# GpSimd masks one score tile of four ahead of its exponential and makes low words; the remaining keys' values come first; the scale moves into query evictions

## The chip, the cores and the metric

The kernel runs on one core of one Trainium2 chip. The metric is device time in microseconds. Three timed runs of the kernel before gave 1319.81, 1322.06 and 1323.58 us; the median, 1322.06, is the time to be changed. One further execution was profiled.

In the text, PE is TensorE (PEld its weight loads), DVE is VectorE, ACT is ScalarE, POOL is GpSimd, and SP is the engine whose queue issues nearly all the DMAs. L468 means line 468 of the kernel before.

## The reference

Two layers follow each other. The first is attention in which only scores within tau of their row's maximum count; the second is a feed-forward block with a squared ReLU. All data that the kernel computes with is fp32, but the two weight matrices arrive as 64-bit floats.

```python
# q, k, v: (8, 8, 576, 64) fp32; tau = 0.02
scores = matmul(q, k^T) / 8
thresh = max(scores, axis=-1) - tau
scores = where(scores >= thresh, scores, -1e9)
attn = exp(scores - max(scores))
attn = attn / (sum(attn) + 1e-9)
x = matmul(attn, v)                    # -> reshaped to (4608, 512)
h = maximum(x @ w_in, 0)               # w_in  (512, 2048)
out = (h * h) @ w_out                  # w_out (2048, 512)
```

## The kernel before, in words

**Two stages.** Attention comes first and leaves its result, transposed, in DRAM. The feed-forward stage (hidden layer on L828, output layer on L963, both with a seven-product scheme over 2 x 2 blocks) reads it back. The change touches attention alone.

**Units and periods.** There are 32 pairs of heads. A *unit* is 128 query rows of one pair (two heads, j = 0 and 1); 576 = 4 x 128 + 64, so the last 64 rows of two neighbouring pairs share a unit. That makes 144 units. Function `period(p)` handles two of them, A = 2p and B = 2p + 1, in 72 full periods. Each unit has two score tiles of 128 x 576, one for each head, so a period has four: A0, A1, B0, B1. Work of three ages meets in a period: scores and softmax of A and B, transposes of the weights of the two units before (V and W), and the rest of the transposes (U) and the values product (PV) of the two units before those.

**The order is written out by hand.** The strings PLAIN (L607) and CONVERTING (L611) list the steps of a period; each engine executes its own steps in that order, one after the other, and semaphores tie the engines together. CONVERTING is used in periods 2 to 34, in which one weight chunk of 128 x 512 64-bit floats is turned into fp32 in each period; PLAIN is used elsewhere. The steps are:

| step | engine | what it does | line |
|---|---|---|---|
| SA, SB | PE | scores of unit A (with both units' last 64 keys), then of B | L436 |
| T, eT | PE, ACT | transposes of queries and keys of a coming pair, and their evictions | L399, L404 |
| topA0 ... topB1 | DVE | scores times -1/8 (qscale) out of PSUM into tile s, and their minimum | L453 |
| leastA, leastB | POOL | thresholds: minimum plus tau, 128 x 2 | L460 |
| powA0 ... | ACT | exponential of tile s into tile w | L463 |
| maskA0 ... | DVE | w = (s <= threshold) * w, and its sum | L468 |
| over, inv, spread | POOL, DVE, POOL | sum + 1e-9, reciprocal, and its spreading to 128 x 256, for the units before | L475, L478, L512 |
| U, V, W and eU, eV, eW | PE, ACT | transposes of the weights, and their evictions | L381, L526 |
| PV | PE | values product into PSUM banks 0 and 5 | L551 |
| x | DVE | PV's result times the reciprocal; its stores and coming loads of values are issued behind it | L653 |
| s1, s2 | POOL | one sum of two weight blocks each (128 x 512), from period 35 on, while there are any; s2 only up to period 59 | L122, L125 |
| c1 to c6 | ACT, ACT, POOL, DVE, DVE, POOL | conversion of a chunk: absolute value of the high words, low words to a float's size, clamp, shift, combine, add | L205, L212, L219, L227, L235, L245 |

Before the change c3 to c6 belong to the chunk of the period before.

**What ties the steps.** Scores of a period use the same PSUM banks as PV's result and the tops of the period before: banks 0 and 5 hold tiles A0 and A1 and then PV's result, so SA waits for x. Banks 1 and 4 hold the last 64 keys' scores and the transposes T, so topA0 waits for T, and eT for the tops. Tile s has two buffers, one each for A and B; w has four. U's transposes read w of two periods before, and so a step that writes w waits for U. Function `touch` (L356) keeps these orders by banks. The transposes use one PSUM tile of two banks, so U waits for eV of the period before and V for eU.

**PV's order.** The product adds up five blocks of keys: four of 128 and one of 64 (FULL), in the order 0, 1, FULL, 2, 3. A product over 128 keys uses PE tiles of 128 x 64, one over 64 keys tiles of 64 x 64, the same as scores.

Of the kernel before, what the change touches and what calls it, by code (L numbers as in the profile page):

```python
# [12 lines left out]
U32 = mybir.dt.uint32  # L13
ALU = mybir.AluOpType
# [34 lines left out]
def kernel(  # L49
# [25 lines left out]
    nc = tc.nc  # L75
# [133 lines left out]
    def convert2(m):  # L209
        if m in parts:  # L210
            lo = parts[m][0]
            nc.scalar.activation(out=lo, in_=lo.bitcast(U32), func=AF.Copy, bias=0.0, scale=2.0**-29)  # L212
# [179 lines left out]
    def turn(i, which, spots, other=None):  # L392
# [13 lines left out]

        def then():
            if which:
                blocks = to[1].rearrange("p (t q) -> p t q", q=HALF)
                evicted(nc.scalar.copy, blocks[:, 0::2, :], spots[0], 0, half + REST)  # L410
                evicted(other if other else nc.scalar.copy, blocks[:, 1::2, :], spots[1], 0, half)
                evicted(nc.scalar.copy, to[2].rearrange("p (t q) -> p t q", q=HALF), spots[1], half, REST)
                next_keys(i)
            else:
                for r in range(2):
                    part = to[0][:, ds(r * half, half)].rearrange("p (t q) -> p t q", q=HALF)
                    evicted(nc.scalar.copy, part, spots[r], 0, half)
                if i + 1 < len(pairs):
                    load_q(i + 1)
# [20 lines left out]

    def softmax(n):
# [9 lines left out]
        def top(j):  # L451
            at = 3 * j * BANK + (n % 2 != j) * (2 * BANK - REST)
            made = nc.vector.tensor_scalar(  # L453
                out=s[:, j, :], in0=sc[:, ds(at, S)], scalar1=qscale[:, :], scalar2=None,
                op0=ALU.mult, op1=ALU.min, accum_out=nmx[:, j : j + 1],
            )
            touch("tops", made, at, S)
# [3 lines left out]

        def power(j):
            nc.scalar.activation(  # L463
                out=w[:, int(n % 2 != j), :], in_=s[:, j, :], func=AF.Exp, bias=nmx[:, j : j + 1], scale=-1.0
            )

        def mask(j):
            nc.vector.scalar_tensor_tensor(  # L468
                out=w[:, int(n % 2 != j), :], in0=s[:, j, :], scalar=thr[:, j : j + 1], in1=w[:, int(n % 2 != j), :],
                op0=ALU.is_le, op1=ALU.mult, accum_out=sm[:, j : j + 1],  # L470
            )
# [8 lines left out]
        soft[n] = dict(top=top, least=least, power=power, mask=mask, over=over, inverse=inverse)  # L480
# [58 lines left out]
    def values(m):  # L539

        for n, c in enumerate((0, 1, FULL, 2, 3)):
# [62 lines left out]
    def begun(n):  # L604
        return starts.get(n)

    PLAIN = """  # L607
        SA c3 T topA0 over U eU s1 SB topA1 powA1 leastA topB0 powB0 c1 s2 PV c4 V fetch
        inv spread powA0 c5 topB1 powB1 eT maskA1 x W eV maskA0 leastB c2 c6 eW maskB0 maskB1
    """.split()  # L610
    CONVERTING = """  # L611
        fetch c3 SA c1 SB topA1 over s1 U topA0 c2 powA1 topB0 topB1 eU leastA maskA1
        leastB inv spread powA0 PV powB0 W maskA0 x powB1 maskB0 T c4 c5 maskB1 eT V c6 eW eV
# [8 lines left out]
    def period(p):  # L622
# [51 lines left out]
        def every(key):  # L674
# [17 lines left out]
        for letter, n in (("A", A), ("B", B_)):  # L692
            for what, name in (("least", "least"),):
                steps[what + letter] = lambda n=n, name=name: do(n, name)
            for what, name in (("top", "top"), ("pow", "power"), ("mask", "mask")):
                for j in range(2):
                    steps[f"{what}{letter}{j}"] = lambda n=n, name=name, j=j: do(n, name, j)
# [528 lines left out]
```

## Time and profile before

| | us |
|---|---|
| median of three timed runs (1319.81 to 1323.58) | 1322.06 |
| profiled execution, whole time | 1318.88 |
| profiled execution, its span | 1317.1 |
| PE busy (matmuls) | 1275.0 |
| DVE busy | 1027.7 |
| ACT busy | 843.7 |
| POOL busy | 883.7 |
| first matmul of the feed-forward stage starts | 522.9 |

The granted TensorE clock was 0.999 of full speed over the whole execution.

How to read it: busy times are those of one execution and averages over stages with different limits. Matmuls are pipelined and the profile models their ends, so that a busy PE is not yet a full PE. A group's line gives busy time, the mean of one in ns, and the engine's idle time just before the group with what ended it. In a timeline, start and length come first; a record that is longer than its kind usually is was held up after it began. Spans on POOL are rough.

### The profile page before, as it was taken

Reading aid. Unit: us, or ns where it says so; the run is one execution under the profiler, and the core shown is the slowest. Engines: PE = TensorE matmul, PEld = TensorE weight load, DVE = VectorE, ACT = ScalarE, POOL = GpSimd, SP = SyncE. Lnnn points to the kernel's source line nnn. Section 1 sums busy time; section 2 is a strip of 40 time slices with the busy share of each in tenths; the row PEclk is TensorE's granted clock in tenths of the full one; section 3 lists DMA queues with packets and bytes.
Section 4 is the critical chain, followed back from the end, with each engine's and each line's share of the span. In section 5 each row is a group of like instructions: output and inputs, shape, how many; then the busy total and the mean of one; then the engine's idle time right before and its main releaser. Section 6 shows DMA issues by size and latency. Waiting matters only on the chain.

```text
span 1317.1 us, 40939 instructions
## 1 busy us (share of the span) xinstructions
PE 1275.0 (97%) x16059; PEld 1116.0 (85%) x16059; DVE 1027.7 (78%) x2497; ACT 843.7 (64%) x1464; POOL 883.7 (67%) x1030
## 2 busy tenths in 40 slices
PE   7898888899999999999999999999999999999998
PEld 5665656566666666999999999999999999999998
DVE  6999999999999997777877787777656644665463
ACT  5999999888988886466756675665524322432240
POOL 1555555566666431778977897768777777777775
PEclk9999999999999999999999999999999999999999
DMA  5454566543433321466556655659745134523411
GB/s 146 128 161 134 156 176 178 152 109 95 112 78 89 79 60 46 135 217 193 184 177 216 193 187 179 204 215 392 266 161 159 50 114 161 161 59 104 161 34 33
DMA packets 251233, 192.73 MB, mean 146 GB/s; under 512 B 103456, under 2 KB 203808, under 8 KB 251040
## 3 DMA queue, kind: packets, MB, share of 16 engines
q1 hardware_dynamic: 249536, 189.66, 46.9%
q8 instruction: 126, 2.06, 0.7%
q10 hardware_dynamic: 1504, 0.46, 0.1%
q14 instruction: 67, 0.55, 0.1%
HBM read 117.70 MB, written 72.35 MB: 144 GB/s over the span
## 4 chain that ended last, share of the span: by engine, by line
PE 82%; DVE 8%; ACT 5%; issue 2%; POOL 1%; DMA 1%; DVEq 0%; POOLq 0%; ACTq 0%
PE ph L828 30%; PE po L963 29%; PE sc L436 9%; PE sc L551 8%; PE pt L381 4%; DVE arena L453 4%; DVE arena L468 3%; ACT arena L463 3%; PE sc L399 1%; POOL arena L512 1%; PE sc L381 1%; ACT arena L526 1%; DVE arena L235 1%; DMA wall<-w 1%; ACT arena L404 1%
## 5 line engine op out<-in xcount | busy, mean ns | idle before, releaser
L125 POOL TENSOR_TENSOR arena<-arena 128x512 f32<-128x512 f32 (+1 forms) x314 | 378.0, 1223 | 131.3 <-DVE arena L125 117.1
L963 PE MATMUL po<-wall,arena 128*128 128x128 f32 x3528 | 394.8, 275 | 1.4 <-ACT arena L740 1.4
L963 PEld LDWEIGHTS po<-wall,arena 128*128 128x128 f32 x3528 | 394.3, 192 | 1.8 <-ACT arena L740 1.8
L828 PE MATMUL ph<-arena,wall 128*128 128x128 f32 x3528 | 394.2, 275 | 0.4 <-DVE arena L653 0.4
L828 PEld LDWEIGHTS ph<-arena,wall 128*128 128x128 f32 x3528 | 394.0, 192 | 0.6 <-DVE arena L653 0.6
L125 DVE TENSOR_TENSOR arena<-ph,arena 128x512 f32<-128x512 f32 x378 | 256.4, 689 | 86.2 <-PE ph L828 65.2
L122 POOL TENSOR_TENSOR arena<-arena 128x128 f32<-128x128 f32 (+2 forms) x314 | 255.3, 814 | 50.9 <-DMA arena<-w 34.8
L125 DVE TENSOR_TENSOR arena<-po,arena 128x128 f32<-128x128 f32 x378 | 108.3, 290 | 168.0 <-PE po L963 163.5
L468 DVE SCALAR_TENSOR_TENSOR arena<-arena 128x576 f32<-128x576 f32 x288 | 228.5, 814 | 0.8 <-ACT arena L463 0.7
L453 DVE TENSOR_SCALAR_CACHE_REDUCE arena<-sc,qscale 128x576 f32<-128x576 f32 x288 | 221.8, 812 | 8.4 <-PE sc L399 2.1
L463 ACT ACTIVATE arena<-arena 128x576 f32<-128x576 f32 x288 | 208.7, 778 | 15.9 <-DVE arena L453 7.0
L774 ACT COPY c<-arena 128x512 f32<-128x512 f32 (+1 forms) x303 | 173.5, 579 | 50.0 <-DVE arena L122 43.3
L551 PEld LDWEIGHTS sc<-arena 128*64 128x64 f32 (+1 forms) x3200 | 141.5, 135 | 72.7 <-DVE arena L453 45.3
L551 PE MATMUL sc<-arena 128*64 128x128 f32 (+3 forms) x3200 | 184.5, 272 | 11.7 <-DVE arena L453 10.6
L122 DVE TENSOR_TENSOR arena<-arena,c 128x512 f32<-128x512 f32 (+1 forms) x267 | 174.9, 663 | 5.9 <-ACT c L774 4.0
L436 PE MATMUL sc<-arena 64*64 64x64 f32 (+1 forms) x2304 | 168.2, 417 | 4.7 <-ACT arena L404 4.7
L526 ACT COPY arena<-pt 128x1024 f32<-128x1024 f32 x144 | 147.3, 1023 | 27.4 <-PE pt L381 27.0
L740 ACT COPY arena<-po 128x128 f32<-128x128 f32 x63 | 16.6, 264 | 186.5 <-PE po L963 183.7
L740 ACT COPY arena<-ph 128x512 f32<-128x512 f32 x63 | 36.6, 581 | 123.0 <-PE ph L828 122.6
L381 PEld LDWEIGHTS pt<-ident,arena 64*128 64x128 f32 x2304 | 83.0, 138 | 37.8 <-ACT arena L526 23.7
L460 POOL TENSOR_SCALAR arena<-arena,tau_p 128x2 f32<-128x2 f32 x144 | 65.9, 458 | 65.5 <-DVE arena L453 61.5
L436 PEld LDWEIGHTS sc<-arena 64*64 64x64 f32 x2304 | 58.6, 134 | 53.3 <-issue 24.8
(44 smaller groups left out, 907.7 us busy)
## 6 DMA issues: line engine op xcount, KB each, us to landing
g<-arena SPq DMA_DIRECT2D x144, 256.0 KB, 2.5
arena<-g SPq DMA_DIRECT2D x144, 256.0 KB, 4.5
w<-arena SPq DMA_DIRECT2D x60, 256.0 KB, 2.4
wall<-w SPq DMA_DIRECT2D x49, 256.0 KB, 5.2
arena<-w SPq DMA_DIRECT2D x44, 256.0 KB, 3.3
out_dram<-arena SPq DMA_DIRECT2D x70, 128.0 KB, 2.3
arena<-in_q_dram SPq DMA_DIRECT2D x64, 128.0 KB, 2.9
arena<-in_v_dram SPq DMA_DIRECT2D x64, 128.0 KB, 2.4
```

The source lines that it names most:

```text
L122: e.tensor_tensor(out=out, in0=x, in1=y, op=ALU.subtract)
L125: e.tensor_tensor(out=out, in0=x, in1=y, op=ALU.add)
L381: made = nc.tensor.transpose(pt[:, r, ts(slot, HALF)], of[rows, :], ident[rows, rows])
L436: made = nc.tensor.matmul(sc[at, ds(to, count)], lhs, kT[rows, ds(at_k, count)], start=True, stop=True)
L453: made = nc.vector.tensor_scalar(out=s[:, j, :], in0=sc[:, ds(at, S)], scalar1=qscale[:, :], scalar2=None, op0=ALU.mult, op1=ALU.min, accu ...
L463: nc.scalar.activation(out=w[:, int(n % 2 != j), :], in_=s[:, j, :], func=AF.Exp, bias=nmx[:, j : j + 1], scale=-1.0)
L468: nc.vector.scalar_tensor_tensor(out=w[:, int(n % 2 != j), :], in0=s[:, j, :], scalar=thr[:, j : j + 1], in1=w[:, int(n % 2 != j), :], op0 ...
L526: touch("weights", nc.scalar.copy(joined(to), whole(pt, 0, count)), at, 2 * BANK, m)
L551: made = nc.tensor.matmul(sc[ds(j * D, D), ds(5 * u * BANK + row, count)], lhs, rhs, start=(n == 0 and s == 0), stop=(n == FULL), skip_gro ...
L774: nc.scalar.copy(c, y)
L828: nc.tensor.matmul(to[:, j, :], W_IN[m, k][:, ts(j, P)], of[k][:, m - 1, :], start=(not more and j == 0), stop=True, skip_group_check=True,)
L963: nc.tensor.matmul(to, g[:, j, :], w[:, j, :], start=(not more and j == 0), stop=(j == 3), skip_group_check=True)
```

## The change

Five things change, all in attention.

- **Mask of A1 on GpSimd.** For tile A1 of each period, two new steps on POOL take the place of the DVE mask: `above` makes (s > threshold) * 1e30 in the tile of weights, and `lift` adds s to it. The exponential comes after them, of minus that sum, so that masked-out scores go to zero, and it gives out the row's sum itself (accum_out). The DVE keeps maskA0, maskB0 and maskB1.
- **c2 on GpSimd.** The low words are scaled by a tensor_scalar on POOL instead of an activation on ACT.
- **Scale in the query evictions.** The factor -1/8 (qscale) is applied in eT as queries leave PSUM, by an Identity activation with a scale per partition instead of a copy; the tops multiply by the constant 1.0.
- **Values of the 64 remaining keys first.** PV's order is FULL, 0, 1, 2, 3.
- **New orders.** Both step lists are written anew. c3, c4 and c5 now follow c1 in the same period, and c6 comes in the next.

```diff
     def convert2(m):
         if m in parts:
             lo = parts[m][0]
-            nc.scalar.activation(out=lo, in_=lo.bitcast(U32), func=AF.Copy, bias=0.0, scale=2.0**-29)
+            nc.gpsimd.tensor_scalar(out=lo, in0=lo.bitcast(U32), scalar1=2.0**-29, scalar2=None, op0=ALU.mult)
...
+        def scaled(to, from_):
+            return nc.scalar.activation(out=to, in_=from_, func=AF.Identity, scale=qscale[:, :])
...
-                evicted(nc.scalar.copy, to[2].rearrange("p (t q) -> p t q", q=HALF), spots[1], half, REST)
+                evicted(scaled, to[2].rearrange("p (t q) -> p t q", q=HALF), spots[1], half, REST)
...
-                    evicted(nc.scalar.copy, part, spots[r], 0, half)
+                    evicted(scaled, part, spots[r], 0, half)
...
+    def by_pool(n, j):
+        return (n % 2, j) == (0, 1)
...
-                out=s[:, j, :], in0=sc[:, ds(at, S)], scalar1=qscale[:, :], scalar2=None,
+                out=s[:, j, :], in0=sc[:, ds(at, S)], scalar1=1.0, scalar2=None,
                 op0=ALU.mult, op1=ALU.min, accum_out=nmx[:, j : j + 1],
...
+        of = lambda j: w[:, int(n % 2 != j), :]
+
+        def above(j):
+            nc.gpsimd.tensor_scalar(
+                out=of(j), in0=s[:, j, :], scalar1=thr[:, j : j + 1], scalar2=1e30, op0=ALU.is_gt, op1=ALU.mult
+            )
+
+        def lift(j):
+            plus(nc.gpsimd, of(j), s[:, j, :], of(j))
+
         def power(j):
-            nc.scalar.activation(
-                out=w[:, int(n % 2 != j), :], in_=s[:, j, :], func=AF.Exp, bias=nmx[:, j : j + 1], scale=-1.0
-            )
+            if by_pool(n, j):
+                nc.scalar.activation(
+                    out=of(j), in_=of(j), func=AF.Exp, bias=nmx[:, j : j + 1], scale=-1.0, accum_out=sm[:, j : j + 1]
+                )
+                return
+            nc.scalar.activation(out=of(j), in_=s[:, j, :], func=AF.Exp, bias=nmx[:, j : j + 1], scale=-1.0)
...
-        for n, c in enumerate((0, 1, FULL, 2, 3)):
+        for n, c in enumerate((FULL, 0, 1, 2, 3)):
...
     PLAIN = """
-        SA c3 T topA0 over U eU s1 SB topA1 powA1 leastA topB0 powB0 c1 s2 PV c4 V fetch
-        inv spread powA0 c5 topB1 powB1 eT maskA1 x W eV maskA0 leastB c2 c6 eW maskB0 maskB1
+        fetch SA T over topA0 U topA1 eU leastA SB aboveA1 powA0 topB0 topB1 inv spread leastB PV
+        powB0 maskA0 eT liftA1 s1 powB1 V x maskB0 W eV s2 maskB1 eW powA1
     """.split()
     CONVERTING = """
-        fetch c3 SA c1 SB topA1 over s1 U topA0 c2 powA1 topB0 topB1 eU leastA maskA1
-        leastB inv spread powA0 PV powB0 W maskA0 x powB1 maskB0 T c4 c5 maskB1 eT V c6 eW eV
+        fetch SA c6 T over topA0 U topA1 eU leastA SB aboveA1 powA0 topB0 c1 topB1 inv spread leastB PV
+        powB0 maskA0 eT c3 c4 liftA1 powB1 c5 V x maskB0 W eV c2 maskB1 eW powA1
     """.split()
...
-            "c1": lambda: convert1(begun(p)), "c2": lambda: convert2(begun(p)),
-            "c3": lambda: convert3(begun(p - 1)), "c4": lambda: convert4(begun(p - 1)),
-            "c5": lambda: convert5(begun(p - 1)), "c6": lambda: convert6(begun(p - 1)),
+            "c1": lambda: convert1(begun(p)), "c2": lambda: convert2(begun(p)), "c3": lambda: convert3(begun(p)),
+            "c4": lambda: convert4(begun(p)),
+            "c5": lambda: convert5(begun(p)), "c6": lambda: convert6(begun(p - 1)),
```

More of the change, by code (lines that the diff above doesn't have):

```diff
@@ L478, in inverse @@
             nc.vector.reciprocal(out=small[:, 3, :], in_=small[:, 2, :])
-        soft[n] = dict(top=top, least=least, power=power, mask=mask, over=over, inverse=inverse)
+        soft[n] = dict(top=top, least=least, above=above, lift=lift, power=power, mask=mask, over=over, inverse=inverse)
     def do(n, what, *args):
@@ L694, in period @@
                 steps[what + letter] = lambda n=n, name=name: do(n, name)
-            for what, name in (("top", "top"), ("pow", "power"), ("mask", "mask")):
+            for what, name in (("top", "top"), ("above", "above"), ("lift", "lift"), ("pow", "power"), ("mask", "mask")):
                 for j in range(2):
```

2 lines of the change are left out of this document (1 added, 1 removed).

## The prediction

> **What bounds the kernel now.** I read the page first (PE 97% busy, DVE 78%, POOL 67%), then the busy times by stretch, the chain of waits inside one stretch, the groups kept apart by shape, and the timeline around single GpSimd instructions. The change lies in attention alone, which ends where the first L828 matmul starts, at 522.9 us; the feed-forward stage behind it stays as it is.
>
> Attention runs in 72 periods, each beginning with the first of four L453 instructions. From their starts: the 33 converting periods (p = 2 to 34) average 7.49 us, the 36 plain ones timed after them 6.60. The first stretch below is the converting one, the second the plain one; the columns are PE, PEld, DVE, ACT and POOL busy.
> ```profile
> 24.80:271.50 246.70, 220.04 (x4126) 147.77 (x4122) 244.23 (x690) 224.40 (x368) 134.67 (x195) 1.00 0.55 152
> 271.50:508.60 237.10, 235.57 (x4456) 159.17 (x4452) 233.11 (x683) 209.50 (x327) 131.32 (x201) 1.00 0.33 84
> ```
> DVE is busy 99% and 98%, PE 89% and 99%. The chain of waits in a plain stretch (start, us, what) tells which one leads:
> ```profile
> 401.57 1.25 PE sc L436 x24
> 402.82 0.39 PE sc L399 x8
> 403.22 0.50 PE pt L381 x16
> 403.71 1.02 PE sc L436 x8
> 404.73 2.56 PE sc L551 x56
> 407.30 0.64 PE pt L381 x16
> 407.94 0.25 PE sc L381 x8
> 408.19 1.25 PE sc L436 x24
> ```
> It never leaves PE: 1.25+0.39+0.50+1.02+2.56+0.64+0.25 = 6.62, the whole period. In a converting stretch the same view goes through L453, L468, L227 and L235, so there DVE leads. GpSimd has half of both stretches free. Whether it can use that time depends on what it meets. The groups kept apart by shape give the lengths (busy us, mean ns of one, idle before):
> ```profile
> L468 DVE SCALAR_TENSOR_TENSOR arena<-arena 128x576 f32<-128x576 f32 x288 | 228.5, 814 | 0.8 <-ACT arena L463 0.7
> L125 POOL TENSOR_TENSOR arena<-arena 128x384 f32<-128x384 f32 x62 | 61.7, 1001 | 80.9 <-DVE arena L125 74.0 <-DMA arena<-g 6.9
> L122 POOL TENSOR_TENSOR arena<-arena 128x512 f32<-128x512 f32 x134 | 170.7, 1274 | 10.2
> L219 POOL TENSOR_SCALAR arena<-arena 128x512 f32<-128x512 f32 x32 | 19.6, 611 | 0.0
> L227 DVE TENSOR_SCALAR arena<-arena 128x512 int32<-128x512 int32 x32 | 13.5, 423 | 0.0
> ```
> and three places of the timeline (start, us, engine) the meetings:
> ```profile
> 123.85 0.82 DVE L468 SCALAR_TENSOR_TENSOR arena<-arena 128x576 f32<-128x576 f32 x1
> 124.04 0.79 POOL L460 TENSOR_SCALAR arena<-arena,tau_p 128x2 f32<-128x2 f32 x1 [0.87 <-DVE arena L453]
> 124.68 0.79 DVE L468 SCALAR_TENSOR_TENSOR arena<-arena 128x576 f32<-128x576 f32 x1
> 124.92 0.80 POOL L512 COPY arena<-arena 128x256 f32<-128x256 f32 x1
> ...
> 28.05 1.26 DVE L468 SCALAR_TENSOR_TENSOR arena<-arena 128x576 f32<-128x576 f32 x1 [0.39 <-ACT arena L463]
> 28.09 0.62 POOL L219 TENSOR_SCALAR arena<-arena 128x512 f32<-128x512 f32 x1
> ...
> 273.45 1.28 POOL L122 TENSOR_TENSOR wall<-wall 128x512 f32<-128x512 f32 x1
> 274.38 0.96 DVE L468 SCALAR_TENSOR_TENSOR arena<-arena 128x576 f32<-128x576 f32 x1
> ```
> A DVE mask (L468, two SBUF inputs) and a GpSimd instruction exclude each other. L460 takes 0.29 elsewhere, but 0.79 when it starts inside a mask: it ends 0.16 after the mask's record. L512 takes 0.40 elsewhere and here ends 0.25 after its mask. The other way round, the mask at 28.05 took 1.26, 0.45 too long: L219 held it up for all but 0.17 of its 0.62. The mask at 274.38 lost 0.15 to a sum with 0.35 left, so a sum lets go 0.2 before its end. The L453 tops read PSUM and run beside sums at their usual length. The present order keeps the sums s1 and s2 beside tops; the two GpSimd instructions that do meet masks are short.
>
> **The change part by part.**
>
> *Mask A1 leaves DVE.* One L468 of four, 0.74 from start to start: 72 x 0.74 = 53 us of DVE time, the whole gain on offer.
>
> *above and lift on GpSimd.* above has one input: by L219, 0.61 x 576/512 = 0.69. It runs beside tops, covered; a compare might be slower, and up to about 1.5 it stays there. lift has two inputs: by 1.00 at 384 and 1.27 at 512, 1.41 at 576, of which it holds masks back for 1.21. Where it falls decides the period, since spread, leastB and (when converting) c3 stand in front of it on POOL.
>
> *A plain period, from topA0 = 0.* Tops at 0, 0.74, 1.48, 2.22; inverse 2.96; maskA0 3.05 to 3.86. spread becomes ready inside maskA0 and ends 3.86 + 0.25 = 4.11; leastB 4.40; lift starts there, holding until 5.61. x fits in at 3.8. maskB0 needs leastB's threshold, but lift, next on the same queue, is already running, as L219 at 28.09 was ahead of its mask: maskB0 waits to 5.61. Queued behind it are maskB1 and the next period's tops, on which scores' banks and PV wait. If s1 is due, it queues at 5.81 during maskB0, starts as that lets go at about 6.28 and holds maskB1 to 7.36; that ends its turn at 8.10. Without a sum it is 5.61 + 2 x 0.74 = 7.09. s2 then falls beside tops. So 8.1 with sums (p = 35 to 65: 56 steps, 2 a period up to p = 59), 7.1 without.
>
> *A converting period.* The same up to leastB 4.40; c3 0.61, to 5.01; lift to 6.42, holding to 6.22. c4 (L227) waits for c3 and finds lift running. Bounds: it is held like a mask, or passes like a top; its operands lie in SBUF like a mask's, so I hold it: 6.22 to 6.68 (0.46 from start to start at L227). Then c2 on POOL, priced by L219 at 0.61 (an integer input may make it 1.0), gets in from 6.5 to about 6.95, c5 (0.61) follows to 7.56, x (0.41) to 7.97. c6 needs c5 alone, starts near 7.7 and, at 0.9 (its 1.48 less the 0.58 it now spends blocked), holds maskB0 to 8.6: two masks end the turn at 10.1. PE's path agrees: x's record ends 8.05, scores 1.25, T to topA0 0.64, 10.0. I take 10.0. If c4 passes, it ends 0.4 earlier and c5 then waits for lift: 9.5.
>
> The Trainium skill, page "SBUF — State Buffer", section "Who interferes with whom", calls the port pair that VectorE shares with GpSimd an exclusive lock, taken by instructions with two SBUF inputs and also by tensor_scalar in its two-port mode. The masks above agree; no run here shows L227 beside GpSimd. By that rule c4 is held and the period is 10.0; were only two-input instructions held, the sum would be 33 x 0.5 = 16 us less.
>
> *c2 leaves ACT*: 32 x about 0.66 = 21 us of ACT, which leads nowhere; no gain. *Scale in the evictions* (96 of them): L463, with a pointer operand, takes 0.78 for 576, L526 0.61 for 512, or 0.66 at the same rate; so at most 0.12 each, 0.15 a period, and the accumulator of powA1 perhaps 0.1 as on DVE (L468's read, 0.08). ACT was busy 209.5 of 237.1 and periods grow: covered; uncovered, 18 us. *Tops with a constant*: from 0 to -0.06 each (a 512 add from PSUM on L125 takes 0.69, 0.76 at 576, against 0.81); I take 0 and keep 288 x 0.06 = 17 us for the low end. *Remaining keys first in PV*: two changes of tile shape fewer, each with 0.17 idle in the weight loads before it: up to 0.3 of PE a period, 22 us, worth something only while PE leads. It no longer would: zero. *Moved DMA issues* (fetch earlier in the plain order, matters only for p = 0 and 1; stores and loads with x): they are issued a period or more ahead, and SP waits on nothing in the chain; zero, at most one late load.
>
> *Sum.* Converting 33 x (10.0 - 7.49) = 83; with sums 31 x (8.1 - 6.60) = 46; the other eight 8 x 0.5 = 4. Together +133. The profiled execution took 1318.88 us (span 1317.1); 1318.9 + 133 = 1452, and the median of the three shown runs is 3 above it: 1455.
>
> **The rivals.**
>
> *GpSimd and DVE block each other only in part.* A sum may not get in between two masks that follow each other directly (no pair of rows shows it): 31 periods of 7.1 instead of 8.1, -31; c4 free, -16; tops at -17. Together 1391; with one of them 1424 to 1439.
>
> *lift holds nothing back.* Against it stands the 28.05 row. Plain periods then go to PE's 6.62 - 0.3 plus a little, 6.5; converting ones still lose, because x now stands behind c4 and c5 on DVE: c3 ends at 4.55, c4 5.1, c5 5.7, x 6.15, PE to the next topA0 1.9: 8.1. 33 x 0.6 - 37 x 0.1 = +16: 1338.
>
> *Faster.* The freed 0.74 reaches the end: converting 7.49 - 0.74, plain PE's 6.3: -33 x 0.74 - 37 x 0.3 = -36, 1287. For it: the busy shares, and PE's two saved shape changes. It needs lift to land in the 3 us of tops; the point is maskB0's delay: under about 0.3 us in plain periods and x no later than now. spread and leastB, which precede lift, end after tops by 1.1 us in the sum above, which speaks against it. That the change does not do what it says gets no chance: the changed program has above and lift on POOL and three masks a period on DVE.
>
> **How the numbers follow.** Forecast 0.66, partial blocking 0.16, no blocking 0.11, faster 0.06, a balance within 0.3% (4 us, what this kernel's runs can tell) 0.01. Below 1385 lie the last three, 0.18; the forecast's upper end adds c2 at 1.0 (33 x 0.4 = 13) and uncovered evictions, about 1483. Range 1385 to 1482. Faster 0.06, same 0.01, slower 0.93.
>
> **What the changed profile would show.** First L828 matmul near 655 instead of 522.9. Period starts 10 apart, then 8. L488 (the masks) well over 0.81 on the mean, about 1.5; L227 over 1 instead of 0.42, or unchanged if it passes; lift at 1.41 straight behind leastB or c3. PE busy down to about 70% of attention. The forecast is wrong if L488 stays at 0.81, or if lift runs beside the tops.

## The result, and the profile after

The changed kernel takes 1530.15 us (median of four runs, 1529.0 to 1532.36) against 1320.93 for the kernel before on the same chip: 1.158 times as long, 95% interval 1.156 to 1.161. The sign of the forecast was right, its size was not: +133 us were forecast and +209 came, outside the range that ended at 1482.

All of it is in attention. The first matmul of the feed-forward stage, now on line 848, starts at 732.9 us; before it started at 522.9. Mean periods, from one topA0 to the next:

| us | converting, p = 2 to 34 | two sums, p = 35 to 59 | one sum, p = 60 to 65 | no sum, p = 66 to 70 |
|---|---|---|---|---|
| before | 7.49 | 6.62 | 6.60 | 6.53 |
| forecast | 10.0 | 8.1 | 8.1 | 7.1 |
| after | 11.80 | 8.60 | 8.39 | 7.52 |

33 x 4.31 = 142 us come from converting periods and 25 x 1.98 + 6 x 1.79 = 60 from those with sums; some 7 are left for the rest. Line numbers shift: masks are L488 now (L468 before), tops L459 (L453), scores L439 (L436), x L673 (L653), PV L571 (L551), least L466 (L460), spread L532 (L512), above L472, lift L125 at 576 columns.

The busy times by stretch of the kernel after (columns PE, PEld, DVE, ACT and POOL busy, then granted clock, DMA share, GB/s), a converting stretch and a plain one:

```profile
34.90:426.90 392.00, 283.94 (x4194) 205.07 (x4190) 295.64 (x637) 219.87 (x374) 288.63 (x297) 0.79 0.36 98
435.40:640.50 205.10, 169.11 (x2972) 113.69 (x2968) 183.61 (x404) 149.02 (x244) 194.83 (x190) 0.99 0.28 70
```

DVE still has the most in the converting stretch, but its 75% is now partly waiting inside instructions; in the plain stretch POOL is busy 95%. PE fell from 89% and 99% to 72% and 82%, and a number stands there that was 1.00 before: the granted clock of the converting stretch is 0.79. The groups of the kernel after, kept apart by shape (busy us, mean ns, idle before):

```profile
L488 DVE SCALAR_TENSOR_TENSOR arena<-arena 128x576 f32<-128x576 f32 x216 | 268.1, 1264 | 30.2 <-POOL arena L466 30.2
L472 POOL TENSOR_SCALAR arena<-arena 128x576 f32<-128x576 f32 x72 | 159.9, 2220 | 6.9
L125 POOL TENSOR_TENSOR arena<-arena 128x576 f32<-128x576 f32 x72 | 101.0, 1403 | 0.0
L122 POOL TENSOR_TENSOR wall<-wall 128x512 f32<-128x512 f32 x33 | 57.6, 1760 | 0.6
L212 POOL TENSOR_SCALAR arena<-arena 128x512 int32<-128x512 uint32 x32 | 51.7, 1616 | 2.9
L227 DVE TENSOR_SCALAR arena<-arena 128x512 int32<-128x512 int32 x32 | 51.6, 1613 | 41.3 <-POOL arena L219 41.3
```

216 masks cost 268 us where 288 cost 228.5. lift takes 1.40, as forecast (1.41). c4 on L227 is held: 1.61 instead of 0.42. Two GpSimd operations are far from their price: above takes 2.22 (taken at 0.69) and c2 1.62 (taken at 0.61 to 1.0). One converting period of the kernel after, from its timeline (start, us, engine; the bracket is the idle time before and what ended it):

```profile
204.50 0.76 DVE L459 TENSOR_SCALAR_CACHE_REDUCE arena<-sc 128x576 f32<-128x576 f32 x1 [0.86 <-PE sc L399]
...
205.25 1.98 PE L439 MATMUL sc<-arena 64*64 64x512 f32 x8
...
206.43 2.22 POOL L472 TENSOR_SCALAR arena<-arena 128x576 f32<-128x576 f32 x1
...
207.34 0.76 DVE L459 TENSOR_SCALAR_CACHE_REDUCE arena<-sc 128x576 f32<-128x576 f32 x1 [1.40 <-ACT arena L485]
...
208.94 0.90 POOL L532 COPY arena<-arena 128x256 f32<-128x256 f32 x1 [0.29 <-DVE arena L498]
...
210.66 1.40 POOL L125 TENSOR_TENSOR arena<-arena 128x576 f32<-128x576 f32 x1
210.73 1.61 DVE L227 TENSOR_SCALAR arena<-arena 128x512 int32<-128x512 int32 x1 [1.14 <-POOL arena L219]
...
212.15 1.61 POOL L212 TENSOR_SCALAR arena<-arena 128x512 int32<-128x512 uint32 x1
212.43 0.96 DVE L235 SCALAR_TENSOR_TENSOR arena<-arena 128x512 int32<-128x512 int32 x1
...
213.32 0.47 DVE L673 TENSOR_TENSOR arena<-sc,arena 128x128 f32<-128x128 f32 x2
...
213.65 1.67 PE L439 MATMUL sc<-arena 64*64 64x512 f32 x6 [3.38 <-DVE arena L673]
213.72 0.80 DVE L488 SCALAR_TENSOR_TENSOR arena<-arena 128x576 f32<-128x576 f32 x1
213.85 1.57 POOL L245 TENSOR_TENSOR wall<-arena 128x512 int32<-128x512 int32 x1
...
214.45 1.58 DVE L488 SCALAR_TENSOR_TENSOR arena<-arena 128x576 f32<-128x576 f32 x1
```

The middle is what the forecast describes: lift holds c4, c5 (L235) runs inside c2 and takes 0.96 instead of 0.70, x comes last, c6 (L245) holds a mask for 0.78. What it lacks stands at the two ends. PE stands still for 3.38 us before the next scores, and at 205.25 the eight scores of SB, which took 1.02 before, take 1.98. Short stretches of the same timeline tell why (the columns are those of the stretches above):

```profile
200.00:201.00 1.00, 0.00 (x0) 0.00 (x0) 0.97 (x2) 0.56 (x2) 1.00 (x1) 0.68 0.00 0
206.00:207.00 1.00, 1.00 (x8) 0.24 (x4) 0.00 (x0) 1.00 (x2) 0.86 (x2) 0.50 0.00 1
208.00:209.00 1.00, 1.00 (x24) 1.00 (x21) 1.00 (x6) 0.85 (x2) 0.71 (x2) 1.00 0.00 0
212.00:213.00 1.00, 0.00 (x0) 0.00 (x0) 0.91 (x2) 0.87 (x2) 0.91 (x2) 1.00 0.00 0
213.00:214.00 1.00, 0.35 (x4) 0.35 (x8) 1.00 (x4) 0.00 (x0) 0.92 (x2) 1.00 0.03 8
214.00:215.00 1.00, 1.00 (x8) 0.52 (x6) 1.00 (x3) 0.00 (x0) 1.00 (x1) 0.50 0.25 72
218.00:219.00 1.00, 1.00 (x20) 0.58 (x14) 0.58 (x3) 1.00 (x2) 0.45 (x2) 1.00 1.06 241
```

PE is without work from 197.8 to 201.25 and from 210.3 to 213.65, 3.4 us each time. The granted clock is 0.50 from 200.4 to 207.2 and from 214.0 to 217.4, so that PE works 5.9 and 3.4 us at half speed. Scores and the transposes T fall in there, and the tops wait for them. The other converting periods look the same: once in each the clock falls, in turn for 6.8 and for 3.4 us. The Trainium skill, page "TensorE: Matmul & The Clock Gate", section "What's actually happening", states half the clock after at least one idle window of some 3.4 us, and the full one after at least one such window of sustained work. This trace agrees in the second, with 5.9 and 3.8 us from the first work to the full clock; the falls come 2.5 and 3.7 us after PE's last work, the first of them sooner than that rule has it, and there the measurement decides.

A plain period with two sums, from the timeline of the kernel after:

```profile
503.35 2.22 POOL L472 TENSOR_SCALAR arena<-arena 128x576 f32<-128x576 f32 x1
...
504.17 0.78 DVE L488 SCALAR_TENSOR_TENSOR arena<-arena 128x576 f32<-128x576 f32 x1
...
505.63 0.40 POOL L532 COPY arena<-arena 128x256 f32<-128x256 f32 x1
...
506.27 1.41 POOL L125 TENSOR_TENSOR arena<-arena 128x576 f32<-128x576 f32 x1
506.34 1.96 DVE L488 SCALAR_TENSOR_TENSOR arena<-arena 128x576 f32<-128x576 f32 x1 [0.81 <-POOL arena L466]
507.63 3.53 POOL L122 TENSOR_TENSOR wall<-wall 128x512 f32<-128x512 f32 x2
...
508.23 1.81 DVE L488 SCALAR_TENSOR_TENSOR arena<-arena 128x576 f32<-128x576 f32 x1
```

This is the forecast's timetable, 0.5 later (0.8 later behind the reciprocal, which comes 0.3 early): lift holds maskB0 and s1 gets in between maskB0 and maskB1. The delay stands in front of it. The reciprocal started at 504.08, but spread, which waits for it, starts at 505.63, when above has ended. POOL's own queue has become long: over 0.23, least 0.29 and 0.30, above 2.22, spread 0.40, lift 1.41 and two sums 3.53 are 8.4 of the 8.6. One thing in these lines contradicts the theory as I had it: maskA0 at 504.17 runs inside above and is not held, 0.78. That is so for all 52 masks that lie wholly inside an above (0.78 to 0.81); lift, the sums and c6 hold masks, the comparison does not.

### The profile page after: what moved, and what is told of

Same layout as the page of the kernel before. It is cut to its first block, busy times and chain, and to the rows that moved or that the text cites. A ratio compares the mean times of both kernels' runs of the same rounds, so it can differ in the third digit from the quotient of the medians.

```text
span 1527.7 us, 41133 instructions
## 1 busy us (share of the span) xinstructions
PE 1353.7 (89%) x16059; PEld 1183.9 (77%) x16059; DVE 1113.3 (73%) x2353; ACT 850.8 (56%) x1504; POOL 1180.3 (77%) x1206
## 4 chain that ended last, share of the span: by engine, by line
PE 60%; POOL 16%; DVE 11%; issue 9%; ACT 1%; DMA 1%; DVEq 0%; SPq 0%; POOLq 0%; ACTq 0%
PE ph L848 26%; PE po L983 24%; POOL arena L472 6%; PE sc L439 4%; DVE arena L488 4%; PE sc L571 3%; DVE arena L227 3%; POOL arena L532 2%; POOL arena L125 2%; POOL arena L466 2%; DVE arena L459 2%; POOL wall L122 2%; PE pt L381 1%; DVE arena L673 1%; POOL arena L219 1%
## 5 line engine op out<-in xcount | busy, mean ns | idle before, releaser
L125 POOL TENSOR_TENSOR arena<-arena 128x512 f32<-128x512 f32 (+2 forms) x386 | 478.7, 1255 | 132.6 <-DVE arena L125 115.2
L439 PE MATMUL sc<-arena 64*64 64x64 f32 (+1 forms) x2304 | 226.0, 511 | 110.0 <-DVE arena L673 109.1
L125 DVE TENSOR_TENSOR arena<-ph,arena 128x512 f32<-128x512 f32 x378 | 256.0, 688 | 86.4 <-PE ph L848 66.2
L488 DVE SCALAR_TENSOR_TENSOR arena<-arena 128x576 f32<-128x576 f32 x216 | 268.1, 1264 | 30.2 <-POOL arena L466 30.2
L571 PEld LDWEIGHTS sc<-arena 128*64 128x64 f32 (+1 forms) x3200 | 157.3, 139 | 125.5 <-DVE arena L459 101.0
L459 DVE TENSOR_SCALAR_CACHE_REDUCE arena<-sc 128x576 f32<-128x576 f32 x288 | 203.2, 750 | 55.7 <-PE sc L399 28.9
L125 DVE TENSOR_TENSOR arena<-po,arena 128x128 f32<-128x128 f32 x378 | 108.0, 289 | 168.1 <-PE po L983 163.8
L571 PE MATMUL sc<-arena 128*64 128x128 f32 (+3 forms) x3200 | 187.3, 269 | 46.4 <-DVE arena L459 46.0
L439 PEld LDWEIGHTS sc<-arena 64*64 64x64 f32 x2304 | 92.7, 164 | 171.5 <-DVE arena L673 102.6
L485 ACT ACTIVATE arena<-arena 128x576 f32<-128x576 f32 x216 | 166.6, 776 | 64.3 <-DVE arena L459 64.0
L472 POOL TENSOR_SCALAR arena<-arena 128x576 f32<-128x576 f32 x72 | 159.9, 2220 | 6.9
L466 POOL TENSOR_SCALAR arena<-arena,tau_p 128x2 f32<-128x2 f32 x144 | 42.2, 293 | 92.0 <-DVE arena L459 89.8
L381 PE MATMUL pt<-ident,arena 64*128 64x64 f32 x2304 | 110.6, 243 | 2.2 <-ACT arena L546 1.6
```

The source lines that it names most:

```text
L125: e.tensor_tensor(out=out, in0=x, in1=y, op=ALU.add)
L439: made = nc.tensor.matmul(sc[at, ds(to, count)], lhs, kT[rows, ds(at_k, count)], start=True, stop=True)
L459: made = nc.vector.tensor_scalar(out=s[:, j, :], in0=sc[:, ds(at, S)], scalar1=1.0, scalar2=None, op0=ALU.mult, op1=ALU.min, accum_out=nmx ...
L472: nc.gpsimd.tensor_scalar(out=of(j), in0=s[:, j, :], scalar1=thr[:, j : j + 1], scalar2=1e30, op0=ALU.is_gt, op1=ALU.mult)
L485: nc.scalar.activation(out=of(j), in_=s[:, j, :], func=AF.Exp, bias=nmx[:, j : j + 1], scale=-1.0)
L488: nc.vector.scalar_tensor_tensor(out=of(j), in0=s[:, j, :], scalar=thr[:, j : j + 1], in1=of(j), op0=ALU.is_le, op1=ALU.mult, accum_out=sm ...
```

## The experiments

The theory after this reading: what decides is, as forecast, that DVE masks and GpSimd exclude each other (the port, for short); on top come the halved clock and the price of the comparison. Rivals: the port plays no part and the new orders are slow by themselves; or the two extra terms are beside the path. All times below are medians; ratios are to the kernel before on the same chip.

**One input per mask** (kernel after; the masks on DVE read w alone, so that they scale it and mask nothing).

```diff
-            nc.vector.scalar_tensor_tensor(
-                out=of(j), in0=s[:, j, :], scalar=thr[:, j : j + 1], in1=of(j),
-                op0=ALU.is_le, op1=ALU.mult, accum_out=sm[:, j : j + 1],
+            nc.vector.tensor_scalar(
+                out=of(j), in0=of(j), scalar1=thr[:, j : j + 1], scalar2=None,
+                op0=ALU.mult, op1=ALU.min, accum_out=sm[:, j : j + 1],
```

> The changed kernel, but the three DVE masks read one tensor from SBUF: they scale the exponential's tile by the threshold and no longer read s, so the masking itself is left out. Length, partitions, accumulator and waits on powX and the threshold stay. Port theory (masks and GpSimd exclude each other because a mask reads two SBUF tensors): masks return to about 0.75 us, a plain period is then set by GpSimd's own queue (0.23+0.29+2.22+0.40+0.30+1.41+2x1.28 = 7.4 us with two sums) instead of 8.6, about 6.6 where there is one sum or none instead of 8.4 and 7.5, and a converting period loses spread's 0.5 us wait: 25x1.1 + 6x1.8 + 5x0.9 + 33x0.5 = 59 us less, about 1470 us. Rival, that only the length of the GpSimd queue in front of the thresholds counts: masks stay as they are in length and the time stays at 1530 us.

Measured: 1474.75 us, ratio 1.116 (1.114 to 1.118); periods 11.36, 7.61, 6.82, 6.45. The groups by shape:

```profile
L488 DVE TENSOR_SCALAR_CACHE_REDUCE arena<-arena 128x576 f32<-128x576 f32 x216 | 167.2, 798 | 51.5 <-POOL arena L466 51.5
L227 DVE TENSOR_SCALAR arena<-arena 128x512 int32<-128x512 int32 x32 | 51.6, 1613 | 30.9 <-POOL arena L219 30.9
```

With one SBUF input a mask is not held any more (0.80, against 1.26), and 55 us go. The 80 masks that start inside lift take 0.81; in the kernel after such masks took 1.94 on the mean. So the second input, or the form of instruction that has it, is what makes masks and lift, sums and c6 exclude each other. c4 has one input too and is held as before, 1.61. The Trainium skill, page "SBUF — State Buffer", section "Who interferes with whom", has a tensor_scalar without an accumulator output, as c4 is, contend with GpSimd in a two-port mode; c4's 1.61 agrees, though no run shows the mode itself. Plain periods are now set by POOL's own queue; converting ones hardly moved.

**PE kept awake** (kernel after; 80 transposes of the identity behind W in converting periods, into columns that nothing reads; the code of the new step F is left out here).

```diff
-        powB0 maskA0 eT c3 c4 liftA1 powB1 c5 V x maskB0 W eV c2 maskB1 eW powA1
+        powB0 maskA0 eT c3 c4 liftA1 powB1 c5 V x maskB0 W F eV c2 maskB1 eW powA1
```

> The changed kernel with 80 transposes of the identity, into columns of banks 1 and 4 that nobody reads, behind W in each converting period: 2.5 us of TensorE work in the 3.4 us in which it waits for x. Clock theory (TensorE idles 3.4 us a period, its granted clock falls to 0.5, scores and their transposes take twice as long in the loop x, SA, T, topA0 and SB, topB0): the granted clock goes to 1.0 in the converting stretch, SA from 2.5 back to 1.25 us, the period from 11.9 to about 9.9 us: 33x2.0 = 66 us less, about 1465 us. Rival, that the port alone makes the extra 2 us: no change, 1530 us, or more where the filler delays SA.

Measured: 1495.91, ratio 1.132 (1.130 to 1.134), mean clock 0.996. Extra work makes the kernel 34 us faster, 1.06 a converting period, about half of what was expected. What takes over shows in the timeline:

```profile
203.42 2.22 POOL L472 TENSOR_SCALAR arena<-arena 128x576 f32<-128x576 f32 x1
...
204.21 0.17 DVE L498 RECIPROCAL arena<-arena 128x4 f32<-128x4 f32 x1
...
205.71 0.40 POOL L532 COPY arena<-arena 128x256 f32<-128x256 f32 x1
```

At full clock the tops are done sooner, and spread now starts 1.5 us behind the reciprocal in the converting periods, since above is in front of it. At half clock it was 0.7 on the mean, 0.3 and about 1.1 in turn.

**No comparison in above** (kernel after; minimum and maximum instead, so that no mask is made in A1).

```diff
-                out=of(j), in0=s[:, j, :], scalar1=thr[:, j : j + 1], scalar2=1e30, op0=ALU.is_gt, op1=ALU.mult
+                out=of(j), in0=s[:, j, :], scalar1=thr[:, j : j + 1], scalar2=1e30, op0=ALU.min, op1=ALU.max
```

> The changed kernel with above as a minimum and a maximum instead of a comparison and a product (so masking of tile A1 is left out): the form of L219, which takes 0.61 us for 512. Theory: above's 2.22 us is a matter of the comparison and falls to 0.7; in a plain period spread, leastB, lift and the two masks behind come 0.5 us earlier (8.6 to 8.1), and in a converting one nothing changes, since above ends there before spread's input is ready: 31x0.5 + 5x0.4 = 17 us less, about 1513 us. Rival, that above is on the path in the converting periods too: 33x1.5 more, about 1465 us. If above stays at 2.2 us it is not the comparison.

Measured: 1495.94, ratio 1.132 (1.129 to 1.134); 34 us less than the kernel after. The group of above by shape:

```profile
L472 POOL TENSOR_SCALAR arena<-arena 128x576 f32<-128x576 f32 x72 | 53.5, 743 | 6.9
```

The same operands at 0.74 instead of 2.22: the pair of a comparison and a product costs three times the pair of a minimum and a maximum, and 0.69 would have been a good price for the latter. Both operations were exchanged at once, so the run does not part the comparison from the product. 34 us is twice the 17 expected: plain periods fall by 0.82 (two sums) instead of 0.5. Converting ones fall by 0.12 only; there the clock is still low, 0.945 over the whole execution.

**Both together.** F is put in and the comparison taken out.

> The changed kernel with both of e2 (TensorE kept busy in converting periods) and e3 (above without its comparison, so A1's masking is left out). Each alone took 34 us. If the clock and the length of above are two limits in a row on the same path in converting periods (the filler alone left 10.74 us there, with above ending 1.4 us after the inverse), the two together give more than their sum: above ends before the inverse again, spread to x come 1.3 us earlier, converting about 9.5 us, plain 7.8 as in e3: 1530 - 33x2.3 - 31x0.8 = about 1430 us. If they are independent: 1530 - 68 = 1462 us.

Measured: 1441.86, ratio 1.091 (1.089 to 1.093), periods 10.00, 7.79, 7.65, 6.77. The pair takes 88 us, more than the 34 + 34 of the two alone, which is what two causes on one path give: each hid part of the other. A converting period is now at the forecast's 10.0, in part by luck: the tops end 0.25 earlier than in the sum, and c5, inside c2, takes about 0.3 longer than it would alone. The kernel stands 120.7 above the kernel before: with full clock and above at the price assumed, the forecast's +133 is 12 too high, not 76 too low.

**c2 back on ACT, on top of that.**

```diff
-            nc.gpsimd.tensor_scalar(out=lo, in0=lo.bitcast(U32), scalar1=2.0**-29, scalar2=None, op0=ALU.mult)
+            nc.scalar.activation(out=lo, in_=lo.bitcast(U32), func=AF.Copy, bias=0.0, scale=2.0**-29)
```

> e7 with the low words back on ACT. Theory: c2 on GpSimd takes 1.6 us, three times what L219 suggested, and c6 behind it then holds the last mask; without it c6 starts earlier, c5 is not held: converting 0.3 to 0.5 us shorter than in e7, plain unchanged, so 10 to 17 us under e7. If c2's whole length is on the path: 1.6 us a period, 53 us under e7.

Measured: 1430.5, ratio 1.082 (1.080 to 1.084); 11 us less, 0.37 a converting period, as the smaller of the two expectations had it.

**The mask back on DVE** (kernel after; no above and lift; maskA1 is put where lift was, powA1 ahead of powA0; c2 stays on POOL).

> The changed kernel with the mask of A1 back on DVE, behind maskA0 (plain) and behind c4 (converting), its exponential behind leastA again; no above and lift. All else of the change stays. Port theory: DVE gets 0.74 us more a period and loses its waits for lift, but s1, s2 and c2 still get in between masks: plain about 7.7 instead of 8.6, converting about 10.5 instead of 11.9 because c2 now stands in front of c4 and x stays behind both: 31x0.9 + 33x1.4 = 74 us less, about 1455 us, still far above the kernel before. Rival, that the mask's move alone makes the loss: about 1330 us.

Measured: 1478.77, ratio 1.119 (1.117 to 1.122). Moving the mask to GpSimd costs 51 us, a quarter of the loss; 157 remain without it, which I had not expected to be so much.

**The orders alone** (the same with c2 on ACT as well).

> The changed kernel with the mask of A1 on DVE (as in e4) and the low words back on ACT: no GpSimd work is new, what is left of the change are the step orders, the scale in the evictions and the remaining keys first. e4 took 1478.8 us. Port theory: without c2 on GpSimd (1.8 us there) the masks behind c4 are no longer held; but x still stands behind c4, c5 and two masks on DVE, so the loop x, SA, T, topA0 stays longer than before: converting about 9.5 us against 10.95 in e4 and 7.49 before, plain 8.2 to 6.8 as in e4 since s1 and s2 still meet masks: about 1430 us. Rival, that the order is harmless and GpSimd's new work makes all the loss: about 1320 us.

Measured: 1451.44, ratio 1.100 (1.097 to 1.102), periods 10.17, 8.19, 7.16, 6.77, clock 0.964. With every instruction back on its engine, the two new orders (and the scale and PV's order, below) still cost 130 of the 209 us. From here the order is undone step by step.

**x right behind maskA0** in the converting order, first in the orders alone, then in the kernel after.

```diff
-        powB0 maskA0 eT c3 c4 maskA1 powB1 c5 V x maskB0 W eV c2 maskB1 eW
+        powB0 maskA0 x eT c3 c4 maskA1 powB1 c5 V maskB0 W eV c2 maskB1 eW
```

> e5 (the change's step orders without its new GpSimd work, 1451 us) with one step moved: in converting periods x stands right behind maskA0, ahead of c4, maskA1 and c5 on DVE, as it stood ahead of them in the kernel before. Theory: in the new order x is what closes the long loop x, SA, T, topA0, and TensorE idles behind it until its clock falls: x comes 2.5 us earlier, SA starts behind W, the granted clock stays near 1.0, the converting period falls from 10.2 to about 8.0 us (DVE's own 7.3 us, one wait for c3, one mask held by c6): 33x2.2 = 70 us less, about 1380 us. Rival, that c4's wait for c3 and the ports set the period whatever x does: under 15 us less.

> The changed kernel, all parts in, with x moved as in e9. Theory: the loop over x and the fallen clock go; what stays is DVE's row of waits for GpSimd: tops 2.7, above until 4.0, spread, leastB and c3 until 5.3, lift until 6.5, then c4, c5, c2 in between (1.4) and two masks: about 10.2 us instead of 11.8: 33x1.6 = 53 us less, about 1477 us. If x is the whole of it, the converting period falls to e9's; if the GpSimd waits alone set it, nothing changes.

Measured: 1408.59 in the first (ratio 1.066, 1.064 to 1.069), 43 less, converting periods 10.17 to 8.75; 1481.01 in the second (ratio 1.121, 1.118 to 1.123), 49 less, 11.80 to 10.32. PE's scores wait for x, so x behind c4 and c5 puts POOL's c3 in front of PE. In the first the clock came back to 0.993, in the second only to 0.961. The groups of the second show where the idle time went (PV; in the kernel after the first of these lines reads 278 ns):

```profile
L571 PE MATMUL sc<-arena 128*64 128x128 f32 x2048 | 171.2, 323 | 0.3 <-ACT arena L546 0.3
...
L571 PE MATMUL sc<-arena 64*64 64x128 f32 x512 | 59.6, 318 | 101.5 <-DVE arena L459 101.2
```

PE now waits for the tops, 101 us in all, before PV, and PV runs slow instead of the scores. In most periods of the second the longest time without work is 1.6 to 1.9 us, and the clock falls all the same, for 3.4 us (it is 1.6 us before the fall at 59.7). The first fell short of its 1380; two experiments down follows what its sum had too small.

**The sums beside the tops** (e9 with s1 and s2 moved in the plain order).

```diff
-        fetch SA T over topA0 U topA1 eU leastA SB powA1 powA0 topB0 topB1 inv spread leastB PV
-        powB0 maskA0 eT maskA1 s1 powB1 V x maskB0 W eV s2 maskB1 eW
+        fetch SA T over s1 topA0 U topA1 eU leastA s2 SB powA1 powA0 topB0 topB1 inv spread leastB PV
+        powB0 maskA0 eT maskA1 powB1 V x maskB0 W eV maskB1 eW
```

> e9_order_x_first with the two sums of a plain period back beside the tops: s1 right behind over, s2 right behind leastA, the rest of both orders untouched. If what is left of the plain loss is the sums getting in between masks, periods with two sums fall from 8.19 us to the 6.8 of periods without any, those with one from 7.16 to 6.8, and converting ones stay at 8.75: 25 x 1.39 + 6 x 0.36 = 37, so 1372 us. Rival: the plain loss is the order of the tops and masks themselves (A0 and A1 ahead of PV, x behind two masks), and the sums only fill the gap it leaves: then moving them changes less than 10 us, and 1400 or more is measured.

Measured: 1374.21, ratio 1.040 (1.038 to 1.041); plain periods with sums 8.19 to 6.91 and 7.16 to 6.94. Converting ones read 8.90 instead of 8.75 although nothing in their order changed. The profiles show where the difference lies: in single periods, eight of the 33 at 9.4 to 9.8 here and three in the run before. In these the granted clock is 0.50 for a part (in two more of the run before, too, which take only 8.34 and 8.36). In the one that starts at 139.8 it falls as PV begins; PV takes 3.9 us, x waits 1.24 us for it, and the period is 9.61. Why the clock falls in these periods and not in their neighbours stays open. The group of sums is back at its length of before, where the kernel after has 1760:

```profile
L122 POOL TENSOR_TENSOR wall<-wall 128x512 f32<-128x512 f32 x33 | 42.2, 1279 | 1.1
```

**c6 beside the tops** (on top of it, in the converting order).

```diff
-        fetch SA c6 T over topA0 U topA1 eU leastA SB powA1 powA0 topB0 c1 topB1 inv spread leastB PV
+        fetch SA T over c6 topA0 U topA1 eU leastA SB powA1 powA0 topB0 c1 topB1 inv spread leastB PV
```

> e11_sums_early with c6 of the converting order moved from behind SA to behind over, beside the tops. If c6 holds maskB1 for 0.78 (its 1.59 where it meets c6, against 0.81), converting periods fall from 8.75 to 8.0, 33 x 0.75 = 25 us below e11_sums_early, so about 1347 us. Rival: the PE path of the period (x, scores of A, the turns, to topA0) takes over at once, and less than 10 us is gained.

Measured: 1346.41, ratio 1.019 (1.017 to 1.020), converting periods 7.94. The timeline with c6 behind SA (e9) has the last mask beside c6:

```profile
216.16 1.48 POOL L245 TENSOR_TENSOR arena<-arena 128x512 int32<-128x512 int32 x1 [1.94 <-ACT arena L212]
...
216.67 1.59 DVE L488 SCALAR_TENSOR_TENSOR arena<-arena 128x576 f32<-128x576 f32 x1
```

and the timeline of this kernel has both at their own length:

```profile
201.38 0.81 DVE L488 SCALAR_TENSOR_TENSOR arena<-arena 128x576 f32<-128x576 f32 x1
...
202.60 1.04 POOL L245 TENSOR_TENSOR arena<-arena 128x512 int32<-128x512 int32 x1
```

So c6 held the mask for 0.78. The 8.0 expected of x right behind maskA0 (e9) had counted such a hold, but left only 0.7 above DVE's own 7.3 for it and for a wait for c3 together; in that timeline the other waits come to about 0.85 (0.2 before maskA0, 0.2 inside it, 0.44 before c4). One way of taking the 209 us apart, each step on top of the one before (their order decides the shares where causes hide each other):

| step undone | median, us | less, us |
|---|---|---|
| the kernel after | 1530.15 | |
| mask A1 back on DVE | 1478.77 | 51 |
| c2 back on ACT | 1451.44 | 27 |
| x ahead of c4 and c5 | 1408.59 | 43 |
| s1, s2 beside the tops | 1374.21 | 34 |
| c6 beside the tops | 1346.41 | 28 |
| the kernel before | 1320.93 | 25 |

The last 25 (33 x 0.45 in converting periods, 36 x 0.3 in plain ones) were not traced further.

**The small parts on the kernel before.** PV's order alone; PV's order with the scale in the evictions; PV's order with tops that multiply by a constant -1/8 and evictions that stay copies.

```diff
-        for n, c in enumerate((0, 1, FULL, 2, 3)):
+        for n, c in enumerate((FULL, 0, 1, 2, 3)):
```

> The kernel before with the remaining keys first alone. TensorE leads the plain periods: two changes of tile shape fewer, at 0.15 us each, so up to 36x0.3 = 10 us less, 1311 us; converting periods unchanged. Rival, that the last blocks' wait for eU or the first one's for topA0 takes the 0.3 us: 1320 us.

> The kernel before with the two small parts of the change alone: the scale in the query evictions (tops with a constant) and the remaining keys' values first. The tops in the changed kernel go 0.68 us from start to start instead of 0.74. Converting periods are led by DVE: four tops, 33x4x0.06 = 8 us less; plain ones by PE: two changes of tile shape fewer, up to 0.3 us, 36x0.25 = 9 us less: about 1305 us, faster than both kernels. If neither is on the path: 1322 us; slower would mean that the evictions on ACT (0.1 us each) delay scores.

```diff
-                out=s[:, j, :], in0=sc[:, ds(at, S)], scalar1=qscale[:, :], scalar2=None,
+                out=s[:, j, :], in0=sc[:, ds(at, S)], scalar1=-SCALE, scalar2=None,
```

> The kernel before with the remaining keys first and with tops that multiply by the constant -1/8 instead of a pointer to it (for tau of zero or more the same numbers; the case of a negative tau is left out); evictions stay plain copies. In b3 the tops went 0.06 us faster, yet the time fell by 0.2% only. Theory: the evictions' extra 0.1 us each on ACT gave it back, ahead of the scores' last part: here the converting period falls to about 7.25 and the plain one to about 6.45: 33x0.24 + 36x0.15 = 13 us less, about 1308 us, faster than both kernels. Rival, that other waits hold the periods (PE, POOL): as b3, 1319 us.

Measured: 1322.30, ratio 1.000 (0.999 to 1.001); 1318.96, ratio 0.999 (0.997 to 1.000); 1316.73, ratio 0.996 (0.995 to 0.998). PV's order gives nothing. The chain of waits in a plain stretch of the first still never leaves PE, and PV keeps its length (2.56 before):

```profile
400.49 1.02 PE sc L436 x8
401.51 2.55 PE sc L551 x40
404.06 0.64 PE pt L381 x16
```

The constant helps the tops: 750 ns on the mean, where qscale as an operand makes it 811 in the same order. Little of that reaches the time: 5 us with plain evictions, 2 with the scale in them. The two intervals touch, so that the loss by the evictions is likely, not shown; scores wait 6.1 us for them, 4.2 in the kernel before. The groups with the scale moved:

```profile
L456 DVE TENSOR_SCALAR_CACHE_REDUCE arena<-sc 128x576 f32<-128x576 f32 x288 | 205.4, 750 | 13.2 <-PE sc L399 3.6 <-ACT arena L529 3.2 <-ACT arena L212 1.7
L439 PE MATMUL sc<-arena 64*64 64x512 f32 x1152 | 158.5, 618 | 6.1 <-ACT arena L408 6.1
...
L408 ACT ACTIVATE arena<-sc,qscale 128x256 f32<-128x256 f32 x62 | 25.7, 469 | 4.1 <-PE sc L399 4.1
```

469 ns for an eviction, 374 as a copy. The third kernel keeps the copies and has the lowest median here, 0.4% ahead of the kernel before.

## Why the prediction was right and wrong

- **The mechanism, right.** Masks and GpSimd hold each other up, in both directions; lift holds maskB0 or c4, s1 gets in between two masks, c6 holds a mask. c2 holds c5 up by 0.26 only, much less than its own length: c5 runs inside it. The one-input run shows the cause for lift, the sums and c6; that masks run unheld inside above was not forecast. "so I hold it" for c4 was right: 1.61, and the Trainium skill's rule on the exclusive port pair (page "SBUF — State Buffer", section "Who interferes with whom") agrees with that number. The rival of partial blocking falls in two of its three parts, c4 passing and no sum between two masks; its third, tops at -0.06, came true.
- **lift 1.41, right** (1.40). **Masks near 1.5 on the mean, L227 over 1, PE near 70%**: 1.26, 1.61, 72% and 82%. The mean of the masks came out lower; maskA0 is held little or not at all (0.79 and 0.78 in the timelines).
- **"I take 10.0" for a converting period: the step that failed first.** The sum had PE's path as "scores 1.25, T to topA0 0.64", lengths of a PE at full clock, though the same sum left PE without work between PV with its transposes and x. It idles 3.4 us, the clock is halved, and the 1.25 became about 2.5. Keeping PE busy with idle work is worth 1.06 a period, and 1.68 once above is out of the way (11.68 to 10.00). With both taken out the period is 10.00.
- **"above has one input: by L219, 0.61 x 576/512 = 0.69 ... up to about 1.5 it stays there": mis-sized.** 2.22. The bound of 1.5 was about right, the price passed it: 0.82 in periods with two sums. The text named a compare as the risk and put no value on it in the range; 31 x 0.8 = 25 us were missing at the upper end.
- **c2, "0.61 (an integer input may make it 1.0)": mis-sized**, 1.62. Its effect was forecast better than its length: without c2 a converting period is 0.37 shorter, and the sum had 0.27 for it (c5 after 6.95 instead of 6.68).
- **Sums: 8.1 with, 7.1 without.** 8.60 and 7.52. Taking away the comparison gives 7.79 and 6.77, both 0.3 below the forecast: four tops at 0.68 from start to start instead of 0.74 are 0.24 of that. The term "I take 0 and keep 17 us for the low end" should have been taken at its end.
- **Remaining keys first, "zero" because PE no longer leads.** Zero, but the reason went untested there; on the kernel before, where PE does lead the plain periods, it is zero as well, against the 0.3 a period that the text allowed. PV there keeps its length (2.55 and 2.56), so the idle times in the weight loads did not lengthen it.
- **What the text did not see** is how much the orders cost alone. It did see x behind c4 and c5, and priced a converting period in which lift holds nothing at 8.1. With no lift, and the mask of A1 back on DVE (0.74), it measured 10.17, with a mean clock of 0.964: there, too, the sum had PE at full clock. The sums between masks it gave as a consequence of lift. They are one of the step lists: with no lift at all a period with two sums takes 8.19.

## What to carry to other kernels

An idle engine's time is only free if what it shares is free: half an idle GpSimd meant little here, because its additions and the DVE masks exclude each other, and moving three of them from beside masks to beside tops that read PSUM was worth 62 us, more than putting the fourth mask back (51). When a sum leaves PE without work for some us (3.4 here, and 1.6 was enough in the kernel after with x moved), price what follows at half clock. Put the price of a new operation (a comparison, an integer input) at a measured row of that operation, or leave the range open to a multiple of its neighbour. Undo a change's order apart from its instructions before putting the loss down to either.

## What the runs showed of the hardware

- Not every GpSimd instruction holds masks up: 52 masks with two SBUF inputs ran wholly inside a GpSimd comparison at 0.78 to 0.81 us (71 more in the run with idle transposes), and the comparison kept its 2.22. c5, which has two SBUF inputs as well, ran inside c2 and was only 0.26 longer. The Trainium skill's rule on the exclusive port pair (page "SBUF — State Buffer", section "Who interferes with whom") agrees with lift, the sums and c6, and not with masks inside the comparison; there the measurement decides.
- A GpSimd tensor_scalar over 128 x 576 takes 2.22 us with a comparison and a multiplication, 0.74 with minimum and maximum.
- A GpSimd scaling of 512 unsigned integers takes 1.62 us, a minimum and maximum of 512 floats (L219) 0.61; ACT does the same scaling in 0.72 (with the copy form of activation).
- With 3.4 us without work in a period the granted TensorE clock fell to 0.50, 2.5 and 3.7 us after the last work in the two periods shown, and was back 5.9 and 3.8 us after work began again. In the kernel after with x moved it fell, in most converting periods, with no more than 1.6 to 1.9 us without work at a time. 80 idle transposes a period brought the mean clock from 0.943 to 0.996 and the kernel 34 us.
- A top from PSUM takes 750 ns with a constant and 811 with a pointer operand; an eviction of 256 columns takes 374 ns as a copy and 469 as an Identity with a scale per partition.
- The accumulator of an activation costs a record of its own of 186 ns (72 of them behind powA1), where a DVE accumulator read takes 79.
